# Where the chunk of three row groups stands among a batch's twelve

## The chip, the cores and the metric

The kernel runs on one core of one Trainium2 chip. The metric is the device time of one execution in microseconds (us), lower is better. Each kernel was timed several times beside runs of the kernel before on the same chip. The chip can differ from one set of runs to the next, so each kernel is compared first with the runs beside it.

## The reference

Cross-covariance attention followed by a gated feed-forward layer, cut to what matters:

```python
# q, k, v: (4, 6016, 256); w_gate, w_val: (256, 1536); w_out: (1536, 256)
qn = q / (norm(q, axis=1) + 1e-6);  kn = k / (norm(k, axis=1) + 1e-6)
a  = softmax(kn.transpose(0, 2, 1) @ qn / tau)          # 256 x 256 per batch
x  = (v @ a).reshape(24064, 256)
out = (sigmoid(x @ w_gate) * (x @ w_val)) @ w_out
```

## The kernel before

A batch has 6016 rows, 47 groups of 128. They are worked on in chunks of four groups, so there are twelve chunks and one of them has three groups. The attention matrix of a batch is multiplied into the two weight matrices once (G and H, "gh" in the code), so a chunk needs only v, transposed. A chunk has 12 slots. In each slot TensorE makes a gate and a value block (`glu`), ScalarE takes the sigmoid of the gate, VectorE multiplies. Between these, TensorE does four matmuls of the output projection of the chunk before it, and "side work": the scores of the next batch, with the squares for its norms on VectorE.

```python
groups = [(t, min(TPC, NT - t)) for t in range(0, NT, TPC)]   # TPC = 4, NT = 47
...
def glu(b, ci, f):
    t0, nt = groups[ci]
    n = nt * P
    ...                       # psg and psv have two PSUM banks each
    for ps, w in ((ps_gate, G), (ps_val, H)):
        for ib in range(CB):
            mm(ps[:, :n], w[f // (FG // P)][:, ib, ...], vT[:, ib, :nt, :], ...)
    nc.scalar.activation(out=g_sb[:, :n], in_=ps_gate[:, :n], func=ACT.Sigmoid)
    nc.vector.tensor_tensor(out=hts[b, ci][:, f, :n], in0=ps_val[:, :n], in1=g_sb[:, :n], op=ALU.mult)
...
for b in range(B):
    for ci in range(NCH):
        block = b + 1 < B and ci in (9, 10)
        for f in range(FC):                       # FC = 12 slots
            glu(b, ci, f)
            flush()                               # VectorE copies a finished output row
            if prev is not None and not block:
                out_mms(*prev, f * TPC, (f + 1) * TPC)
            for fn, a in side.get((ci, f), ()):
                fn(*a)
            if (b, ci) == (0, 0) and f < len(gh_order) - 5:
                gh(0, 5 + f, pso, "o")            # 7 of the 12 G/H products of batch 0
        ...                                       # chunks 9 and 10: output matmuls after the slots
        prev = (b, ci)
```

In the first batch nothing hides the loads. The order of the software queue is q and k of the batch, the first v chunk, then the weights.

Of the kernel before, what the change touches and what calls it, by code (L numbers as in the profile page):

```python
# [17 lines left out]
def kernel(  # L18
# [29 lines left out]
    NT = N // P  # L48
# [4 lines left out]
    TPC = 4  # L53
    CH = TPC * P
    NCH = (NT + TPC - 1) // TPC
    groups = [(t, min(TPC, NT - t)) for t in range(0, NT, TPC)]

    head = NT - NT % TPC
    groups0 = groups[: head // TPC] + [(t, n) for t, n in ((head, NT % TPC - 1), (NT - 1, 1)) if n > 0]

    def rows(x, b):
        return x[b].rearrange("(p t) c -> p t c", p=P)
# [24 lines left out]
    def mm(out, lhsT, rhs, start, stop, **kw):  # L87
        nc.tensor.matmul(out, lhsT=lhsT, rhs=rhs, start=start, stop=stop, **kw)  # L88
# [12 lines left out]
    vs = {}  # L101

    def load_v(b, ci):
        t0, nt = groups[ci]
        v_sb = vpool.tile([P, TPC, C], BF16, tag="v", name="v_sb")
        nc.gpsimd.dma_start(out=v_sb[:, :nt, :], in_=rows(v, b)[:, t0 : t0 + nt, :])  # L106
        vs[b, ci] = v_sb


    t0, nt = groups0[0]  # L110
# [20 lines left out]
    for t0, nt in groups0[2:]:  # L131
        load_qk(0, t0, nt)
    load_v(0, 0)

    w_sb = [[consts.tile([P, CB, FG], BF16, name=f"w_{n}{fg}") for fg in range(NFG)] for n in ("gate", "val")]
    w_out_sb = consts.tile([P, FC, C], BF16)
    for fg in range(NFG):
        for w, src in enumerate((moe_w_gate, moe_w_val)):
            nc.gpsimd.dma_start(
                out=w_sb[w][fg],  # L140
                in_=src.rearrange("(t p) f -> p t f", p=P)[:, :, ds(fg * FG, FG)],
            )
    load_v(0, 1)
    nc.gpsimd.dma_start(out=w_out_sb, in_=moe_w_out.rearrange("(t p) c -> p t c", p=P))

# [239 lines left out]

    def transpose_v(b, ci, ps=None, late=None):

        t0, nt = groups[ci]
        v_sb = vs.pop((b, ci))
        vT = vtpool.tile([P, TPC * CB, P], BF16, tag="vT", name="vT")  # L390
        flat = v_sb[:, :nt, :].rearrange("p t c -> p (t c)")
        if ps is None:
            nc.sync.dma_start_transpose(out=vT[:, : nt * CB, :], in_=flat)
        else:
            for n in range(nt * CB):
                nc.tensor.transpose(  # L396
                    out=ps[:, n, :], in_=flat[:, ds(n * P, P)], identity=ident_bf
                )
            half = nt * CB // 2
            (nc.scalar.copy if late is None else late)(vT[:, half : nt * CB, :], ps[:, half : nt * CB, :])  # L400
            nc.vector.tensor_copy(out=vT[:, :half, :], in_=ps[:, :half, :])
        vts[b, ci] = vT.rearrange("p (u cb) n -> p cb u n", cb=CB)
# [1 line left out]
    hts = {}  # L404

    def glu(b, ci, f):
        t0, nt = groups[ci]
        n = nt * P
        G, H = st[b]["gh"]
        vT = vts[b, ci]  # L410
        if f == 0:
            hts[b, ci] = hpool.tile([P, FC, CH], BF16, tag="hT", name="hT")
        ps_gate = psg.tile([P, CH], FP32, tag="g", name="ps_gate")
        ps_val = psv.tile([P, CH], FP32, tag="v", name="ps_val")
        for ps, w in ((ps_gate, G), (ps_val, H)):
            for ib in range(CB):
                mm(
                    ps[:, :n],
                    w[f // (FG // P)][:, ib, ds(f % (FG // P) * P, P)],
                    vT[:, ib, :nt, :],  # L420
                    start=(ib == 0),
                    stop=(ib == CB - 1),
                )
        g_sb = gpool.tile([P, CH], BF16, tag="g", name="g_sb")
        nc.scalar.activation(out=g_sb[:, :n], in_=ps_gate[:, :n], func=ACT.Sigmoid)  # L425
        nc.vector.tensor_tensor(  # L426
            out=hts[b, ci][:, f, :n], in0=ps_val[:, :n], in1=g_sb[:, :n], op=ALU.mult
        )
# [2 lines left out]

    def out_mms(b, ci, n0, n1):

        t0, nt = groups[ci]
        hT = hts[b, ci]
        for n in range(n0, min(n1, nt * FC)):
            s, f = divmod(n, FC)
            if n == 0:
                ffn[b, ci] = opool.tile([P, TPC, C], FP32, tag="osb", name="out_sb")
            if f == 0:  # L440
                ffn["ps"] = pso.tile([P, C], FP32, tag="o", name="ps_o")
            mm(ffn["ps"], hT[:, f, ds(s * P, P)], w_out_sb[:, f, :], f == 0, f == FC - 1)
            if f == FC - 1:
                pending.append((ffn[b, ci], s, ffn["ps"], b, ci))
# [3 lines left out]
    def flush():  # L448
        while pending:
            out_sb, s, ps, b, ci = pending.pop(0)  # L450
            t0, nt = groups[ci]
            nc.vector.tensor_copy(out=out_sb[:, s, :], in_=ps)  # L452
            if s == nt - 1:
                nc.sync.dma_start(out=out_rows[b][:, t0 : t0 + nt, :], in_=out_sb[:, :nt, :])

    def last_rows(b, ci):

        t0, nt = groups[ci]
        s, half = nt - 1, C // 2
        hT = hts[b, ci]  # L460
        nc.sync.dma_start(out=out_rows[b][:, t0 : t0 + s, :], in_=ffn[b, ci][:, :s, :])
        for n, queue in enumerate((nc.sync, nc.scalar)):
            ps = pso.tile([P, half], FP32, tag="o", name="ps_end")
            for f in range(FC):
                mm(ps, hT[:, f, ds(s * P, P)], w_out_sb[:, f, ds(n * half, half)], f == 0, f == FC - 1)
            end = opool.tile([P, half], FP32, tag=f"end{n}", name="end", bufs=1)
            nc.vector.tensor_copy(out=end, in_=ps)  # L467
            queue.dma_start(out=out_rows[b][:, t0 + s, ds(n * half, half)], in_=end)
# [15 lines left out]
    for g, (t0, nt) in enumerate(groups0):  # L484
# [32 lines left out]
    weights(0, 1)  # L517
    late = []
    transpose_v(
        0, 0, psv.tile([P, TPC * CB, P], BF16, tag="v", name="ps_tp"), lambda *a: late.append(a)  # L520
    )
# [12 lines left out]
    def side_work(b):  # L534
# [7 lines left out]
        for ci in range(NCH):  # L542
            nb, nci = (b, ci + 1) if ci + 1 < NCH else (b + 1, 0)
            lb, lci = (b, ci + 2) if ci + 2 < NCH else (b + 1, ci + 2 - NCH)
            if (nb, nci) == (0, 1):
                at(8, lambda: transpose_v(0, 1, psm.tile([P, TPC * CB, P], BF16, tag="m", name="ps_tp")))
            elif nb < B:
                at(ci * FC + 2, transpose_v, nb, nci)
            if lb < B:
                at(ci * FC + 0, load_v, lb, lci)  # L550
# [33 lines left out]
    for b in range(B):  # L584
        side = side_work(b)
        for ci in range(NCH):
            block = b + 1 < B and ci in (9, 10)
            for f in range(FC):
                glu(b, ci, f)
                flush()  # L590
# [5 lines that stand above are left out]
                    gh(0, 5 + f, pso, "o")  # L596
            if prev is not None and block:
                for s in range(TPC):
                    for fn, a in side.get((ci, FC + s), ()):
                        fn(*a)  # L600
                    out_mms(*prev, s * FC, (s + 1) * FC)
                    flush()
            prev = (b, ci)
    for s in range(groups[NCH - 1][1] - 1):
        out_mms(*prev, s * FC, (s + 1) * FC)
        flush()
    last_rows(*prev)


# [33 lines left out]
```

## Time and profile before

| | before |
|---|---|
| time, median of the first 3 runs | 829.4 us |
| span of the profiled run | 827.7 us |
| TensorE busy | 806.9 us, 97% |
| VectorE, ScalarE busy | 71%, 47% |
| first gate matmul of chunk 1, batch 0, from the start of the span | 53.08 us |
| from there to the end | 774.6 us |

With TensorE busy for 97%, shares tell nothing of a change that moves work about. What can be read is the start of each matmul in the timeline. The next start less the time that the columns between take (0.423 ns a column in this kernel) is a gap. After the first 40 us this kernel has four gaps of 0.04 us or more (0.25, 0.30, 0.30 and 0.07). Where a group in the listing has an odd count, a record is missing, and the apparent gap of one matmul (0.22 us) there is not a real one.

### The profile page before, as it was taken

How to read it: one execution, taken by the hardware profiler on the slowest of the kernel's cores; microseconds unless marked ns; L12 is line 12 of the kernel's file. 1: busy time of each engine (PE TensorE's matmuls, PEld its weight loads, DVE VectorE, ACT ScalarE, POOL GpSimd, SP SyncE). 2: the span in 40 equal slices, each digit the busy share in tenths (PEclk: the TensorE clock that was granted, in tenths of full speed). 3: DMA queues.
4: the chain of work that ended last, by engine and by line, in shares of the span. 5: the costliest groups of instructions: out<-in, count | busy, mean ns of one | idle time of the engine just before them, and what ended most of it. 6: DMA issues, size and time to landing. Idle time of an engine off the chain costs nothing.

```text
span 827.7 us, 13626 instructions
## 1 busy us (share of the span) xinstructions
PE 806.9 (97%) x5122; PEld 498.5 (60%) x5134; DVE 591.5 (71%) x1027; ACT 390.8 (47%) x642; POOL 83.1 (10%) x159
## 2 busy tenths in 40 slices
PE   4799999999999999999999999999999999999998
PEld 2456666665665666665575666666566566666666
DVE  6777877787667777778767777777766666666665
ACT  4554444446644444445654444444655444444442
POOL 5532100002210100000311010000000000000000
PEclk9899999999999999999999999999999999999999
DMA  9999623226746443223876452223322323322211
GB/s 210 206 201 216 110 52 90 60 53 136 158 88 119 96 89 61 54 52 85 158 138 124 80 107 60 51 63 75 64 61 63 73 52 85 60 58 69 47 36 71
DMA packets 79026, 77.17 MB, mean 93 GB/s; under 512 B 50800, under 2 KB 55920, under 8 KB 78960
## 3 DMA queue, kind: packets, MB, share of 16 engines
q0 software_dynamic: 23920, 38.81, 28.1%
q1 hardware_dynamic: 54752, 36.91, 17.4%
q8 instruction: 40, 0.66, 0.3%
q10 hardware_dynamic: 288, 0.59, 0.2%
q14 instruction: 26, 0.21, 0.1%
HBM read 78.64 MB, written 24.64 MB: 125 GB/s over the span
## 4 chain that ended last, share of the span: by engine, by line
PE 94%; DMA 4%; DVE 1%; issue 0%; ACT 0%; POOL 0%; POOLq 0%
PE ps_o L88 30%; PE ps_gate L88 29%; PE ps_val L88 29%; PE ps_s L88 4%; DMA k_sb<-in_k_dram 3%; PE ps_gh L88 2%; DMA w_gate<-in_moe_w_gate_dram 1%; DVE hT L426 0%; ACT g_sb L425 0%; PE ps_end L88 0%; DVE sq L176 0%; PE ps_n L88 0%; POOL q_sb L97 0%; PE ps_tp L396 0%; DVE end L467 0%
## 5 line engine op out<-in xcount | busy, mean ns | idle before, releaser
L426 DVE TENSOR_TENSOR hT<-ps_val,g_sb 128x512 bf16<-128x512 f32 (+1 forms) x576 | 390.8, 679 | 205.6 <-ACT g_sb L425 201.0
L425 ACT ACTIVATE g_sb<-ps_gate 128x512 bf16<-128x512 f32 (+1 forms) x576 | 338.2, 588 | 386.2 <-PE ps_gate L88 380.2
L88 PE MATMUL ps_val<-vT,gh_H 128*128 128x512 bf16 (+1 forms) x1152 | 337.6, 375 | 0.3
L88 PE MATMUL ps_gate<-vT,gh_G 128*128 128x512 bf16 (+1 forms) x1152 | 337.5, 375 | 0.2
L88 PE MATMUL ps_o<-w_out_sb,hT 128*128 128x256 bf16 x2244 | 324.9, 273 | 0.0
L88 PEld LDWEIGHTS <-hT 128*128 128x128 bf16 x2268 | 221.0, 98 | 124.6
L88 PEld LDWEIGHTS <-gh_H 128*128 128x128 bf16 x1152 | 112.7, 98 | 132.1 <-issue 1.4
L88 PEld LDWEIGHTS <-gh_G 128*128 128x128 bf16 x1152 | 112.4, 98 | 37.6 <-ACT gh_G L379 0.2
L106 POOL DMA_DIRECT2D v_sb<-in_v_dram x48 | 25.5, 531 | 620.2 <-DMA vT<-v_sb 480.4
L452 DVE COPY out_sb<-ps_o 128x256 f32<-128x256 f32 x187 | 77.2, 413 | 12.6 <-PE ps_o L88 12.6
L88 PE MATMUL ps_s<-k_sb,q_sb 128*128 128x256 bf16 x376 | 70.5, 289 | 15.8 <-DMA k_sb<-in_k_dram 8.8
L88 PEld LDWEIGHTS <-q_sb 128*128 128x128 bf16 x376 | 38.6, 103 | 24.6 <-issue 9.6
L215 DVE TENSOR_TENSOR acc<-acc,sq 128x1024 bf16<-128x1024 bf16 (+1 forms) x66 | 44.1, 669 | 0.0
L176 DVE TENSOR_TENSOR sq<-q_sb 128x1024 bf16<-128x1024 bf16 (+2 forms) x44 | 29.3, 667 | 0.0
L97 POOL DMA_DIRECT2D q_sb<-in_q_dram x48 | 26.5, 552 | 15.2 <-DMA q_sb<-in_q_dram 7.3
L97 POOL DMA_DIRECT2D k_sb<-in_k_dram x48 | 26.2, 545 | 16.1 <-DMA k_sb<-in_k_dram 6.6
L176 DVE TENSOR_TENSOR sq<-k_sb 128x1024 bf16<-128x1024 bf16 (+2 forms) x34 | 22.4, 658 | 0.2 <-DMA k_sb<-in_k_dram 0.2
L174 ACT ACTIVATE sq<-k_sb 128x1024 bf16<-128x1024 bf16 (+1 forms) x11 | 11.2, 1019 | 13.6 <-DMA k_sb<-in_k_dram 13.6
L88 PE MATMUL ps_gh<-w_val,e_sb 128*128 128x512 bf16 x45 | 13.5, 379 | 0.2
L88 PEld LDWEIGHTS <-e_sb 128*128 128x128 bf16 x112 | 10.2, 98 | 5.3 <-DMA w_gate<-in_moe_w_gate_dram 0.6
L88 PE MATMUL ps_gh<-w_gate,e_sb 128*128 128x512 bf16 x41 | 12.7, 379 | 0.7 <-DMA w_gate<-in_moe_w_gate_dram 0.5
L425 ACT ACT_TABLE_LOAD x6 | 7.7, 1283 | 9.0 <-PE ps_gate L88 9.0
(69 smaller groups left out, 121.1 us busy)
## 6 DMA issues: line engine op xcount, KB each, us to landing
out_dram<-out_sb SPq DMA_DIRECT2D x44, 512.0 KB, 2.9
v_sb<-in_v_dram POOLq DMA_DIRECT2D x44, 256.0 KB, 3.8
q_sb<-in_q_dram POOLq DMA_DIRECT2D x43, 256.0 KB, 7.4
k_sb<-in_k_dram POOLq DMA_DIRECT2D x43, 256.0 KB, 8.1
out_dram<-out_sb SPq DMA_DIRECT2D x3, 384.0 KB, 3.1
w_gate<-in_moe_w_gate_dram POOLq DMA_DIRECT2D x3, 256.0 KB, 8.0
w_val<-in_moe_w_val_dram POOLq DMA_DIRECT2D x3, 256.0 KB, 8.1
w_out_sb<-in_moe_w_out_dram POOLq DMA_DIRECT2D x1, 768.0 KB, 13.3
```

What stands on the lines that cost most here:

```text
L88: nc.tensor.matmul(out, lhsT=lhsT, rhs=rhs, start=start, stop=stop, **kw)
L97: nc.gpsimd.dma_start(out=tl[:, :nt, :], in_=rows(src, b)[:, t0 : t0 + nt, :])
L106: nc.gpsimd.dma_start(out=v_sb[:, :nt, :], in_=rows(v, b)[:, t0 : t0 + nt, :])
L174: nc.scalar.activation(out=sq[:, :nt, :], in_=src[:, :nt, :], func=ACT.Square)
L176: engine.tensor_tensor(out=sq[:, :nt, :], in0=src[:, :nt, :], in1=src[:, :nt, :], op=ALU.mult)
L215: nc.vector.tensor_tensor(out=acc[:, :nt, :], in0=acc[:, :nt, :], in1=st[b]["sq", w][:, :nt, :], op=ALU.add)
L425: nc.scalar.activation(out=g_sb[:, :n], in_=ps_gate[:, :n], func=ACT.Sigmoid)
L426: nc.vector.tensor_tensor(out=hts[b, ci][:, f, :n], in0=ps_val[:, :n], in1=g_sb[:, :n], op=ALU.mult)
L452: nc.vector.tensor_copy(out=out_sb[:, s, :], in_=ps)
```

## The change

The intent is that the partial chunk comes first and the last chunk of each batch is a full one. Loads of q and k keep their groups.

```diff
+    short = NT - (NCH - 1) * TPC
+    chunks = [(0, short)] + [(short + t * TPC, TPC) for t in range(NCH - 1)]
...
     def load_v(b, ci):
-        t0, nt = groups[ci]
+        t0, nt = chunks[ci]
...   (the same line in transpose_v, glu, out_mms, flush and last_rows)
-    for s in range(groups[NCH - 1][1] - 1):
+    for s in range(chunks[NCH - 1][1] - 1):
```

More of the change, by code (lines that the diff above doesn't have):

```diff
@@ L386, in transpose_v @@
     def transpose_v(b, ci, ps=None, late=None):
-        t0, nt = groups[ci]
+        t0, nt = chunks[ci]
         v_sb = vs.pop((b, ci))
@@ L406, in glu @@
     def glu(b, ci, f):
-        t0, nt = groups[ci]
+        t0, nt = chunks[ci]
         n = nt * P
@@ L432, in out_mms @@
     def out_mms(b, ci, n0, n1):
-        t0, nt = groups[ci]
+        t0, nt = chunks[ci]
         hT = hts[b, ci]
@@ L450, in flush @@
             out_sb, s, ps, b, ci = pending.pop(0)
-            t0, nt = groups[ci]
+            t0, nt = chunks[ci]
             nc.vector.tensor_copy(out=out_sb[:, s, :], in_=ps)
@@ L456, in last_rows @@
     def last_rows(b, ci):
-        t0, nt = groups[ci]
+        t0, nt = chunks[ci]
         s, half = nt - 1, C // 2
```

## The prediction

> **What bounds the kernel now.** I read the page's busy times first, then the chain of waits, then the groups with shapes kept apart, and last the timeline at the head, at a batch's edge and at the tail. The first part of the page, and the sums by engine of its chain:
>
> ```profile
> PE 806.9 (97%) x5122; PEld 498.5 (60%) x5134; DVE 591.5 (71%) x1027; ACT 390.8 (47%) x642; POOL 83.1 (10%) x159
> ...
> PE 94%; DMA 4%; DVE 1%; issue 0%; ACT 0%; POOL 0%; POOLq 0%
> ```
>
> TensorE is busy for 97% and carries 94% of the chain; the 4% of DMA is the head, where q and k of the first batch arrive. So the question is not how busy anything is, but where TensorE stands still. Walking the TensorE timeline start by start (the next start minus the columns streamed), I find 19.4 us of gaps. About 16.2 us lie before 38.9 us, nearly all waits for q, k and the first weight. After that the real gaps are 0.25 us at 42.0, 0.30 at 254.0 and 0.30 at 453.5, some of 0.03 to 0.07, and about 2 us that are only missing records (0.21 us, each beside a group with an odd count). The groups by form:
>
> ```profile
> L426 DVE TENSOR_TENSOR hT<-ps_val,g_sb 128x512 bf16<-128x512 f32 x528 | 364.1, 690 | 181.5 <-ACT g_sb L425 179.5 <-PE ps_gate L88 0.4
> L425 ACT ACTIVATE g_sb<-ps_gate 128x512 bf16<-128x512 f32 x528 | 315.1, 597 | 368.4 <-PE ps_gate L88 368.4
> L426 DVE TENSOR_TENSOR hT<-ps_val,g_sb 128x384 bf16<-128x384 f32 x48 | 26.7, 555 | 24.0 <-ACT g_sb L425 21.4 <-PE ps_gh L88 2.2
> L425 ACT ACTIVATE g_sb<-ps_gate 128x384 bf16<-128x384 f32 x48 | 23.1, 487 | 17.8 <-PE ps_gate L88 11.8 <-DVE hT L426 6.0
> ```
>
> The x48 forms are the short chunks, 12 slots in each of 4 batches. ScalarE and VectorE wait for TensorE in both sizes.
>
> **Cost of TensorE work, from starts.** In the steady part pairs of 512-column matmuls start 0.433 us apart, pairs of 384 columns 0.325 and groups of four of 256 columns 0.433. All are 0.423 ns per column, with nothing to see per instruction. A full slot of gate and value is 4 x 0.2165 = 0.866 us, a short one 4 x 0.1625 = 0.650 us, four output matmuls 0.433 us.
>
> **What the Trainium skill says.** "TensorE: Matmul & The Clock Gate", section "Back-to-back issue gap", gives N / 2.4 + 2.5 ns when warm: 215.8, 162.5 and 109.2 ns for 512, 384 and 256 columns. The trace has 216.5, 162.5 and 108.3, so it agrees; the 131 ns that the same section has for a sustained stream at 512 is not met here. "VectorE: DVE Perf Modes", section "The TRN2 errata — SBUF-src ops pay a fixed extra latency per instruction", gives (120 + columns) / 0.96 ns for a PSUM source: 658 and 525 ns; the trace has 690 and 555 for the product, 30 more, but the slope agrees, so a short slot does not take three quarters of a full one's VectorE time. "ScalarE: Activation LUTs", section "What ACT_TABLE_LOAD costs", gives 1283 ns for the load and 1380 for a drain; the trace shows 1283 and the next activation 0.01 us later, so I use 1.28 us. "DMA: Bandwidth & Descriptors", section "Queues, rings and completion order", says that an SDMA engine takes the descriptors of a ring in ring order. The head agrees: k tiles of the same queue land 2.48 us apart (waits ending at 28.31 and 30.79), so a tile issued earlier and made smaller moves up all behind it.
>
> **The change, part by part.** The rows per batch are the same 47. Each batch's chunk 0 loses 12 slots x 4 matmuls x 128 columns x 0.423 ns = 2.60 us of gate and value work and its last chunk gains as much. The output work moves too, and sums to the same. Number and shapes of instructions are unchanged, only their order. For a kernel with TensorE full that is zero, so what is left is four edges.
>
> (1) *Head, the load.* The first v tile is queued before the first weight tile, and that weight is what starts the G/H matmuls:
>
> ```profile
> 28.51 8.00 DMA w_gate<-in_moe_w_gate_dram
> 36.55 0.60 PE ps_gh L88 x2
> ...
> 40.89 0.60 ACT g_sb L425
> 41.51 0.70 DVE hT L426
> 42.26 0.59 PE ps_val L88 x2
> ```
>
> A tile of four rows costs 2.48 / 2 = 1.24 us of the queue, so a row less lands the weight 0.31 us earlier. The first G/H matmul would start at 36.24; its operand e, ready at 35.85, allows it. Six transposes in place of eight save nothing: TensorE waits for e after them.
>
> (2) *Head, the first chunk.* There are no output matmuls yet. After the weight the chain goes through ScalarE: two copies of G and H, the table load 39.59 to 40.87, the sigmoid, the product, and only then the value matmul of slot 2. With all 0.31 earlier and the short forms: sigmoid 40.57 to 41.06, product 41.09 to 41.65, value of slot 2 at 41.71, against 42.26. That is 0.55 us earlier. But TensorE does 5 short pairs (2 slots and a gate) x 0.108 = 0.54 us less before it, so there is no gain: the wait there grows from 0.25 to some 0.4 (and 0.1 at the gate before it). Then the G/H slots: TensorE 0.650 + 0.433 = 1.083 us; VectorE 0.555 + 0.743 / 2 = 0.93 us, ScalarE 0.487 + 0.687 / 2 = 0.83. TensorE bounds them, but the product of slot 1 is behind a G/H scaling, and I allow 0.1 us. The five slots without G/H take 0.650 us. There the loop gate (0.49 from start to end), sigmoid (0.04 + 0.487), product (0.03 + 0.555) and release (0.05) is 1.65 us, while the value matmul two slots on wants its bank 2 x 0.650 + 0.325 = 1.625 us after the gate's start; with full slots it was 2.06. So no slack is left, and the copies of the second chunk's transposes, 0.58 us on ScalarE and 0.42 on VectorE in slot 8, fall into this. I work it out to 0.22 us of wait in slot 11. Sum of (1) and (2): -0.01 + 0.1 + 0.22, about **+0.35 us**.
>
> (3) *Batch edges.* Output matmuls are handed out four a slot, so a predecessor of three rows leaves slots 9 to 11 without any. Today these are in chunk 0:
>
> ```profile
> 252.64 0.41 DVE L452 COPY out_sb<-ps_o 128x256 f32<-128x256 f32 x1
> 252.97 0.68 DVE L176 TENSOR_TENSOR sq<-q_sb 128x1024 bf16<-128x1024 bf16 x1
> 253.57 1.28 DVE L426 TENSOR_TENSOR hT<-ps_val,g_sb 128x512 bf16<-128x512 f32 x2
> ...
> 254.31 0.59 PE L88 MATMUL ps_val<-vT,gh_H 128*128 128x512 bf16 x2
> ```
>
> The last output copy and a square stand ahead of the product of slot 10, whose value bank the next chunk's first slot needs. The gate matmuls before it started at 253.58 and take 0.43, so TensorE loses 0.30 us. This occurs after chunk 0 of batches 1 and 2, and not in batch 3, whose VectorE has no next batch to prepare. After the change the three slots are in chunk 1, with scores and squares in the same slots, and batch 0 has them too. So three losses in place of two: **+0.30 us**. The short chunk 0 of later batches has its 48 output matmuls: TensorE 0.650 + 0.433 + 0.108 (scores) = 1.19 us a slot, VectorE 0.555 + 0.14 (output) + 0.34 (squares) = 1.03, no wait. The last chunk, now full, has the G/H matmuls as well and only gains slack.
>
> (4) *Tail.* The end is the same two half rows, their copies and transfers. One more row of output matmuls stands before them, which the sum counts. The transfer just ahead carries three rows, not two. The page has 2.0 us to landing for 256 KB and 2.9 for 512 KB, so 0.45 us more; it is issued 1.2 us before the last, and some of it may hold that up: **+0.1 us**.
>
> Sum: 0.35 + 0.30 + 0.1 = 0.75 us; 829.4 + 0.7 = **830.1 us**.
>
> **The rivals.** *The head pays.* If the weight 0.31 us earlier, and less work before the wait in slot 2, came out whole, and the short slots ran without the wait that I give them, the time would be about 829. Against it: work taken from chunk 0 comes back in chunk 11, while waits that hang on ScalarE's table load do not shrink with it. *The two-bank loop binds the whole short chunk.* If each of the 12 slots of the first chunk lost 0.1 to 0.15 us, this would make 831 to 831.5. For it is the slack of none in the last five slots; against it that the G/H slots have 0.15 us over VectorE's time. *The edge stalls vanish* rather than move, because chunk 1 meets other neighbours: 0.9 us less than my sum, 829.2; the unchanged slot parity of squares and scores speaks against it. *A late load.* The first DMA transpose takes 16.0 us to land, from 48.84; its chunk starts about 2.3 us earlier than today's 71.5, which leaves some 4 us. Were it late, all of that would be lost; I give it 3%.
>
> **Range and chances.** Each of the four terms can be off by its own size, and runs of the kernel before differ by 0.4 us. 829.1 to 831.2 holds these. A change of 2% is 16.6 us, more than the whole of the idle time after the head, and the head's loads are not shortened by more than 0.31. Faster 0.5%, within 98.5%, slower 1%.
>
> **What would show it.** In the changed profile: first G/H matmul near 36.24; chunk 1's first gate near 50.8 (53.08 today, less 2.60 by work alone would be 50.48); a gap of 0.3 us at the end of chunk 1 in batches 0, 1 and 2 and none at the end of chunk 0; TensorE busy time within 1 us; the same half-row tail. It is wrong if gaps appear inside the later short chunks, or if a transfer ends TensorE's wait after 55 us.

## The result

The changed kernel took 830.40 us (median of 6 runs, 830.02 to 830.76), the kernel before 829.54 (6 runs, 829.36 to 829.76). The ratio is 1.001, 95% interval 0.9997 to 1.0023. A ratio is the mean time of one kernel's runs over that of the other's in the same rounds, so it is not quite the ratio of the medians quoted. No run of either kernel falls in the range of the other.

Busy times and the chain's shares by engine, after:

```profile
PE 807.5 (97%) x5120; PEld 498.5 (60%) x5132; DVE 591.3 (71%) x1027; ACT 390.7 (47%) x642; POOL 83.2 (10%) x159
...
PE 93%; DMA 4%; DVE 1%; ACT 1%; issue 1%; POOL 0%; ACTq 0%; POOLq 0%
```

Nothing to see, as one would expect: the same work. (The two matmuls fewer are missing records.) ScalarE has entered the chain with 1%. The groups by form, after; the columns are busy us and mean ns of one, then idle time ahead and what ended it:

```profile
L429 DVE TENSOR_TENSOR hT<-ps_val,g_sb 128x512 bf16<-128x512 f32 x528 | 364.1, 690 | 190.3 <-ACT g_sb L428 188.6
L428 ACT ACTIVATE g_sb<-ps_gate 128x512 bf16<-128x512 f32 x528 | 314.8, 597 | 361.1 <-PE ps_gate L91 361.0
L429 DVE TENSOR_TENSOR hT<-ps_val,g_sb 128x384 bf16<-128x384 f32 x48 | 26.5, 556 | 16.0 <-ACT g_sb L428 15.7
L428 ACT ACTIVATE g_sb<-ps_gate 128x384 bf16<-128x384 f32 x48 | 23.4, 490 | 24.1 <-DVE hT L429 12.5 <-PE ps_gate L91 11.4
```

Counts and durations are those of before, to 3 ns, so no instruction became dearer. The difference is in waits. The chain through the head, after (start, duration, what; L533 is the sigmoid's table load):

```profile
28.64 7.88 DMA w_gate<-in_moe_w_gate_dram
36.51 0.05 issue
36.56 0.61 PE ps_gh L91 x2
...
38.31 0.69 ACT gh_G L382
39.00 0.58 ACT gh_H L382
39.58 0.02 issue
39.59 1.28 ACT L533
40.88 0.01 issue
40.89 0.50 ACT g_sb L428
41.39 0.02 issue
41.41 0.57 DVE hT L429
41.98 0.04 issue
42.02 0.48 PE ps_val L91 x2
```

Behind the first G/H matmuls and a row sum, up to the value matmul of slot 2, the chain no longer runs over TensorE. It runs over a copy of G and the inverse of that row sum on VectorE (left out above), the two copies on ScalarE, the table load, the sigmoid and the product. It ends 0.24 us earlier than before (42.26), while TensorE has 0.54 us less to do. The batch's edge, after, in the timeline of chunk 1 of batch 0:

```profile
66.06 0.41 DVE L455 COPY out_sb<-ps_o 128x256 f32<-128x256 f32 x1
...
66.39 0.68 DVE L179 TENSOR_TENSOR sq<-q_sb 128x1024 bf16<-128x1024 bf16 x1
...
66.99 1.28 DVE L429 TENSOR_TENSOR hT<-ps_val,g_sb 128x512 bf16<-128x512 f32 x2
67.00 0.59 PE L91 MATMUL ps_gate<-vT,gh_G 128*128 128x512 bf16 x2
...
67.73 0.59 PE L91 MATMUL ps_val<-vT,gh_H 128*128 128x512 bf16 x2
```

This is the pattern of before, copy and square ahead of the product that frees a value bank: 67.00 + 0.43 = 67.43, the value matmul starts at 67.73, 0.30 us are lost. It recurs at 267.8 and 467.3, so three times in place of two.

The account of the two profiled runs, from starts in the timelines:

| stretch | before | after | difference | less the work moved |
|---|---|---|---|---|
| start to the spreading of the k norms (`ps_rk`, a matmul) | 34.16 | 34.33 | +0.17 | (head of the run, untouched) |
| from there to the first G/H matmul | 2.39 | 2.23 | -0.16 | -0.16 |
| from there to chunk 1's first gate | 16.53 | 14.84 | -1.69 | -1.69 + 2.60 = +0.91 |
| from there to the end | 774.62 | 777.40 | +2.78 | +2.78 - 2.60 = +0.18 |

The last +0.18 is the third edge gap of 0.30 less one small gap of 0.07 us (at 606.98 before) that this run has not; the remaining 0.05 is no more than the rounding of the spans to 0.1 us. The sum is 827.7 to 828.8 us of span. The profiled run of the changed kernel is the slowest of its six.

### The profile page after: what moved, and what is told of

Same layout as the page of the kernel before. It is cut to its first block, busy times and chain, and to the rows that moved or that the text cites. A ratio compares the mean times of both kernels' runs of the same rounds, so it can differ in the third digit from the quotient of the medians.

```text
span 828.8 us, 13622 instructions
## 1 busy us (share of the span) xinstructions
PE 807.5 (97%) x5120; PEld 498.5 (60%) x5132; DVE 591.3 (71%) x1027; ACT 390.7 (47%) x642; POOL 83.2 (10%) x159
## 4 chain that ended last, share of the span: by engine, by line
PE 93%; DMA 4%; DVE 1%; ACT 1%; issue 1%; POOL 0%; ACTq 0%; POOLq 0%
PE ps_o L91 30%; PE ps_val L91 29%; PE ps_gate L91 29%; PE ps_s L91 4%; DMA k_sb<-in_k_dram 3%; PE ps_gh L91 2%; DMA w_gate<-in_moe_w_gate_dram 1%; DVE hT L429 1%; ACT g_sb L428 0%; DVE sq L179 0%; PE ps_end L91 0%; ACT L533 0%; PE ps_n L91 0%; DVE gh_G L384 0%; ACT gh_G L382 0%
## 5 line engine op out<-in xcount | busy, mean ns | idle before, releaser
L177 ACT ACTIVATE sq<-k_sb 128x1024 bf16<-128x1024 bf16 (+1 forms) x11 | 11.2, 1018 | 13.6 <-DMA k_sb<-in_k_dram 13.6
```

What stands on the lines that cost most here:

```text
L177: nc.scalar.activation(out=sq[:, :nt, :], in_=src[:, :nt, :], func=ACT.Square)
```

## The experiments

Theory A is the account above: the short first chunk of batch 0 loses 0.91 us in waits and gains a little from an earlier weight; each stretch of slots without output matmuls that also carries squares costs 0.30 us; the rest is neutral. The rivals put the loss in the short chunks of the later batches (B), deny that the gaps cost anything in the end (C), hold slots without output matmuls to be dear by themselves (D), or hold the short chunk to be bound as a whole by its loop of gate, sigmoid, product and freed bank, so that a cured wait comes back elsewhere (E). The differences are below 0.2% for every kernel here. What decides between the theories is therefore where the gaps stand in the one profile of each kernel; the times only have to agree.

**Batch 0 alone has the short chunk first.**

```diff
-    chunks = [(0, short)] + [(short + t * TPC, TPC) for t in range(NCH - 1)]
+    at_front = [(0, short)] + [(short + t * TPC, TPC) for t in range(NCH - 1)]
+    chunks_of = [at_front] + [groups] * (B - 1)        # read as chunks_of[b][ci]
```

> Batch 0 has its short chunk first as in the changed kernel, batches 1 to 3 have it last as before. Theory A (the loss is made of a head term of about 0.75 us in the first chunk and 0.30 us for each stretch of three slots without output matmuls that carries next-batch squares): chunk 1 of batch 0 starts near 51.4 us as in the changed kernel; a 0.30 us gap at the end of chunk 1 of batch 0 and at the end of chunk 0 of batch 2, none in batch 1; two gaps, so about 0.3 us less than the changed kernel and 0.7 more than before, 830.2. Rival B (the loss is spread over the short first chunks of batches 1 to 3, none of it in the head): about 829.6. Rival C (gaps at the edges cost nothing in the end because later slack takes them up): as long as the changed kernel, 830.4.

Measured: 830.15 us median (mean of 5 runs 830.17) beside 829.65 (mean of 9 runs 829.67). The gaps are where A has them: 0.30 us after the group that starts at 66.72, none in batch 1, 0.30 at 453.7. From the first G/H matmul to chunk 1 it is 14.84 us, as in the changed kernel. So the head's loss is in batch 0 and nothing is lost in the later short chunks; B falls. Its median is 0.25 us below the changed kernel's 830.40, where A expects 0.3, but the spreads of the two overlap and they were not run side by side.

**Three output matmuls per slot after a chunk of three.** The same edit in the changed kernel and in the kernel before (there with `groups`):

```diff
-                    out_mms(*prev, f * TPC, (f + 1) * TPC)
+                    rows_prev = chunks[prev[1]][1]
+                    out_mms(*prev, f * rows_prev, (f + 1) * rows_prev)
```

> The changed kernel, with a three-row predecessor's 36 output matmuls handed out three per slot over twelve slots in place of four per slot over nine. Theory A: the three 0.30 us gaps at the end of chunk 1 of batches 0, 1 and 2 are gone and nothing comes in their place, so 0.9 us less than the changed kernel, near 829.5, level with before; chunk 1 still starts near 51.4. Rival C (the gaps cost nothing, or come back as smaller waits in the nine slots that now have one matmul less): no gain, 830.4.

> The kernel before with the same three per slot after a three-row chunk. Theory A: its two 0.30 us gaps (254.0 and 453.5) are gone, 0.6 us less than before, near 828.9. Rival C: no gain, 829.5.

Measured: 829.44 us (829.28 to 829.72) for the changed kernel so edited, 829.05 (828.71 to 829.17) for the kernel before so edited, beside the same 829.65. The 0.30 us gaps are gone in both timelines and none has come in their place. From chunk 1 to the end it is 776.50 us in place of 777.40, and 773.96 in place of 774.62. These are 0.90 and 0.66 us, of which the gaps are 0.90 and 0.60. So the gaps cost their full length, and C falls.

**The short chunk as the eighth of twelve.**

```diff
+    at_7 = [(t * TPC, TPC) for t in range(7)] + [(7 * TPC, short)] + [(7 * TPC + short + t * TPC, TPC) for t in range(NCH - 8)]
+    chunks_of = [at_7] * B
```

> The chunk of three row groups is the eighth of the twelve in each batch, so the slots without output matmuls fall into the last three of the ninth, where VectorE has no next-batch work, and both the head and the tail have full chunks. Theory A (it takes squares in these slots to make the 0.30 us gap): no gap at the batch edges and none in the ninth chunk, head as before (chunk 1 near 53.1), 0.6 us less than before, near 828.9. Rival D (slots without output matmuls lose time by themselves): four gaps of about 0.3 us at the end of the ninth chunks, 830.0 or more.

Measured: 829.09 us (828.77 to 829.16), beside 829.65. The last three slots of the ninth chunk, in batch 0 around 183 to 185 us, have no output matmuls and no squares, and no gap:

```profile
183.50 0.42 DVE L457 COPY out_sb<-ps_o 128x256 f32<-128x256 f32 x1
...
183.83 1.48 DVE L431 TENSOR_TENSOR hT<-ps_val,g_sb 128x512 bf16<-128x512 f32 x2
...
184.22 0.59 PE L93 MATMUL ps_gate<-vT,gh_G 128*128 128x512 bf16 x2
...
184.65 0.60 PE L93 MATMUL ps_val<-vT,gh_H 128*128 128x512 bf16 x2
```

The value matmul follows its gate after 0.43 us, as it should. The output copy is there and does no harm alone. So D falls. That it takes the square as well is read from VectorE's order at the gaps; these slots also lack the next batch's scores, and no run has one without the other. Head and remainder are as A has them: 16.52 us from the first G/H matmul to chunk 1, and 773.97 to the end. This kernel and the kernel before with three per slot have lower medians than both kernels of this study. All their runs lie below all runs of the kernel before, but at 0.07% the intervals (0.998 to 1.0005, and 0.9979 to 1.0004) don't exclude 1.

**The largest new wait of the first chunk.** Within the 0.91 us, the wait that the prediction did not have is in slot 8, after:

```profile
47.36 0.56 DVE L429 TENSOR_TENSOR hT<-ps_val,g_sb 128x384 bf16<-128x384 f32 x1 [0.48 <-ACT g_sb L428]
...
47.84 0.74 DVE L384 TENSOR_SCALAR gh_H<-ps_gh,rrow 128x512 bf16<-128x512 f32 x1
48.12 0.33 PE L91 MATMUL ps_val<-vT,gh_H 128*128 128x384 bf16 x1
...
48.63 0.34 PE L91 MATMUL ps_val<-vT,gh_H 128*128 128x384 bf16 x1 [0.19 <-DVE gh_H L384]
```

Slot 8 is the first to use the last third of H, whose second half is the twelfth G/H product, made in slot 6. Its scaling stands in VectorE's order behind the product of slot 6 and ends at 48.58. The second value matmul could have started 0.16 us after the first, at 48.28, and starts at 48.63: 0.35 us. The experiment makes that product in slot 5, in a free PSUM bank:

```diff
-                if (b, ci) == (0, 0) and f < len(gh_order) - 5:
+                if (b, ci) == (0, 0) and f < len(gh_order) - 6:
                     gh(0, 5 + f, pso, "o")
+                    if f == len(gh_order) - 7:
+                        gh(0, 6 + f, pss, "s")
```

It ran beside the changed kernel itself, which was run once more:

> The changed kernel once more, as the measure for the three beside it on the same chip: 830.4 us, 14.85 us from the first G/H matmul to the first gate matmul of chunk 1.

> The changed kernel with the last of the twelve G/H products made one slot of the first chunk earlier, in a PSUM bank of its own, so that its VectorE copy is done before the value matmul of slot 8 wants it. Theory A (0.33 us of the 0.91 that the short first chunk loses is the wait for that copy): the wait in slot 8 goes, 14.5 us from the first G/H matmul to chunk 1, 0.35 us less than the changed kernel, 830.05. Rival E (TensorE is held by the loop through ScalarE and VectorE as a whole, and the wait in slot 8 is only where it shows): the loss turns up in slots 9 to 11, no gain.

Measured: 830.53 us (mean 830.52) for the changed kernel, 830.20 (mean 830.16) for the edit, beside 829.68 for the kernel before. From the first G/H matmul to chunk 1 it is 14.51 us in place of 14.84. The wait in slot 8 is gone, and slot 11 waits 0.20 us as before. So the 0.33 us were a wait of their own, and E fails for it. The medians differ by the same 0.33 us, with overlapping spreads.

**The size of the first v load.**

```diff
+        ld = TPC if (b, ci) == (0, 0) else nt
-        nc.gpsimd.dma_start(out=v_sb[:, :nt, :], in_=rows(v, b)[:, t0 : t0 + nt, :])
+        nc.gpsimd.dma_start(out=v_sb[:, :ld, :], in_=rows(v, b)[:, t0 : t0 + ld, :])
```

> The changed kernel, but the first v load brings four row groups as before, of which three are used. If the smaller load is worth 0.31 us, as the prediction had it, the first G/H matmul comes 0.31 us later counted from the spreading of the k norms than in the changed kernel run beside it, and the time is 0.3 us more; from the traces so far (2.25 to 2.39 us with four rows, 1.76 to 2.30 with three) some 0.2 us, and the time the same within what five rounds can tell.

Measured: 830.89 us (mean 830.78) beside 830.53 (mean 830.52) of the changed kernel, with overlapping spreads. From the spreading of the k norms to the first G/H matmul it took 2.29 us here and 1.77 in the changed kernel beside it. Over all the profiles, four rows gave 2.39, 2.25, 2.29 and 2.29 us, three rows 2.23, 2.30, 1.76, 2.37, 1.77 and 1.77. The means are 2.31 and 2.03, a difference of 0.27 us, but it comes as half a microsecond or nothing. The landings in the traces say more. Counted from the spreading of the k norms, the v tile lands at -0.19 to -0.21 us with four rows and at -0.45 to -0.53 with three: some 0.29 earlier, close to the 0.31 predicted. The weight behind it does not follow: it lands at 2.20 to 2.35 with four rows, at 2.18 to 2.33 in three of the profiles with three rows, and at 0.80 to 0.83 in the other three. The same transfer with three rows, in the changed kernel's first profile (issued at 28.64) and its second (28.53):

```profile
w_gate<-in_moe_w_gate_dram POOLq DMA_DIRECT2D x1, 256.0 KB, 7.9
w_gate<-in_moe_w_gate_dram POOLq DMA_DIRECT2D x1, 256.0 KB, 6.4
```

So the weight is 1.4 us earlier or not at all, and of the 1.4 only half a microsecond is used, because the first matmul on the operand e does not start before 1.70 in any profile. What decides which was not found. Nor is it shown that the row less has a part in it: three in six against none in four is what chance alone gives one time in six (an estimate, 20 of the 120 ways to place three).

**All cures in one.** Three per slot, the twelfth product in slot 5, and the transposes for chunk 1 moved from slot 8 to the slot that it left:

```diff
-                at(8, lambda: transpose_v(0, 1, psm.tile(...)))
+                at(6, lambda: transpose_v(0, 1, psm.tile(...)))
```

> The changed kernel with three cures together: output matmuls of a three-row predecessor three per slot, the last G/H product one slot earlier, and the transposes for chunk 1 in slot 6 in place of slot 8. Theory A: 0.90 + 0.33 + 0.21 us of gaps go, 829.0, so that the short chunk first is no longer dearer than last; 14.3 us from the first G/H matmul to chunk 1. Rival E: only the 0.90 goes, 829.5.

Measured: 829.43 us (mean 829.50), beside 829.68 for the kernel before and 830.53 for the changed one. This is a miss by 0.4 us, and E's number. The trace tells two reasons. The transposes cost slot 9 the same 0.20 us that they had cost slot 11 (14.47 us from the first G/H matmul to chunk 1, not 14.3), so for this wait E was right. And there is a new wait at the first gate of chunk 3, for a DMA that landed late. The timeline of this kernel, and the DMA view's issue-to-landing time (last column) of the transpose issued at 68.91:

```profile
68.91 1.75 SPq L396 DMA_TRANSPOSE vT<-v_sb  x1
...
83.52 0.11 PEld L91 LDWEIGHTS <-gh_G 128*128 128x128 bf16 x2 [0.41 <-DMA vT<-v_sb]
```

```profile
vT<-v_sb SPq DMA_TRANSPOSE x1, 14.6
```

68.91 + 14.6 = 83.5 us. In the kernel before the same transpose is issued at 72.77 and takes 10.8, landing at 83.6; in the changed kernel it is 66.98 + 16.5 = 83.5; with the changed kernel's three per slot 69.30 + 13.6 = 82.9. It lands at nearly one time, whenever it is issued (82.9 to 84.0 in all ten profiles), while the DMA engines are full with the next batch's q and k (their share is 1.0 to 1.1 in this stretch in both kernels). Before, chunk 3 starts at about 87.1, 3.5 us later. In the changed kernel it starts at about 84.4, less than 1 us later, and in the kernel with the twelfth product in slot 5 only 0.3 us later. In this one it would have started at 83.23, and loses 0.30.

## Why the prediction was right

It was right: 830.4 us against 830.1, inside the range. The edges came out as reasoned, and so did the head's waits as far as it saw them. That the sum is so close has luck in it: a wait of 0.35 us that it did not see is as large as its whole term for the head, and was in part made up by a tail term that came to nothing and a small gap that went.

- **The work is conserved.** Shown: durations and counts are unchanged, and every difference found is a wait. TensorE's busy time is within the 1 us given (806.9 and 807.5).
- **(1) The weight comes 0.31 us earlier.** Right for the v tile (some 0.29), not shown for the weight. The first G/H matmul was 0.16 earlier in the profiled run and 0.27 on the average of ten profiles, but each profile shows one of two places and not a shift by 0.31: it was at 36.56 in the profiled run and at 35.95 in the repeated one, on either side of the 36.24 expected. So the step from "in ring order" to "moves up all behind it" failed: the section that the prediction cites for the order also says that a later transfer can finish its write before an earlier one, and here the place in the queue did not fix the time of landing.
- **(2) The first chunk.** The waits came to 0.91 us from the first G/H matmul on; the prediction's figures amount to some 0.62. (Its sum -0.01 + 0.1 + 0.22 is 0.31, which it rounded up to 0.35.) Up to slot 2 it has 0.30 (0.54 of work less, 0.24 of time, from 0.55 less the load's 0.31), and 0.29 was measured. The 0.1 it allowed for the G/H slots was 0.04. The 0.22 of slot 11 was 0.20. What it lacked is the 0.35 us of slot 8. It checked G/H slots for throughput, VectorE's 0.93 us against TensorE's 1.083, and not for the deadline of the last product, which short slots bring closer. So the term of +0.35 us measured 0.91 less what the load gave: 0.75 in the profiled runs, and 0.91 - 0.27 = 0.64 with the average of the profiles. Two slips change nothing in the sum: the lines that it shows have VectorE wait for ScalarE's sigmoid (179.5 of 181.5 us), not for TensorE directly, and with full slots the bank is wanted 2 x 0.866 + 0.433 = 2.165 us after the gate's start, not 2.06.
- **(3) Batch edges, +0.30.** Right to the hundredth, with places and batches. That the stalls move rather than vanish was shown, no gap came inside the later short chunks, and the spreading and the eighth-chunk kernels bear out the cause.
- **(4) Tail, +0.1.** Wrong: nothing. From the issue of the last transfer to the end of the span it is 827.7 - 824.83 = 2.87 us before and 828.8 - 825.94 = 2.86 after. The larger transfer ahead did not hold up the last one.
- **Sum.** 0.64 + 0.30 + 0, and -0.12 for the rest of the last stretch, is 0.82 us; the medians differ by 0.86, and by 0.85 when the changed kernel was run again.
- **The rivals.** *The head pays* and *the edge stalls vanish* did not happen. *The two-bank loop binds the whole short chunk* has a grain of truth: slots 9 to 11 have no slack, and a wait cured there comes back. *A late load* was nearer than the 3% given it suggests: the transpose to watch was the second, not the first, with less than 1 us to spare. The prediction's 4 us for the first is a misreading: its chunk, chunk 2, starts at 69.99 before, not at 71.5, and at 67.00 after. It comes 3.0 us earlier, not 2.3, because a chunk of three rows also leaves its successor 12 x 0.108 = 1.3 us less of output work. The transpose landed at 64.74, so 2.3 us were left. No transfer ended a wait of TensorE after 55 us in the changed kernel.

## What to carry to other kernels

Where one engine is full and the work is only reordered, add up the waits at the few edges where its neighbours have no slack: shrinking work there gains less than its size (1.69 of 2.60 us here), and the same work comes back in full elsewhere. In this kernel the partial chunk did best where the slots that it leaves without filler carry no other engine's extra work, or with its filler spread evenly over the slots; each took some 0.6 us off the median. When slots shrink, check deadlines as well as throughput: operands made a fixed number of slots ahead, and transfers that land at one time however early they are issued.

## What the Trainium skill lacked or had wrong

- "TensorE: Matmul & The Clock Gate", section "Back-to-back issue gap": the 131 ns per matmul of 512 columns in a sustained stream is not met; 216.5 ns in all of this kernel, with weight loads between, which is the page's figure for a single gap.
- "ScalarE: Activation LUTs", section "What ACT_TABLE_LOAD costs": no drain of 1380 ns shows. The load takes 1.28 us from 39.59 and the sigmoid starts at 40.88 in the kernel before and 40.89 in the changed one.
- "VectorE: DVE Perf Modes", section "The TRN2 errata — SBUF-src ops pay a fixed extra latency per instruction": the table's 120 cycles are too few for a product from PSUM; 690 ns at 512 columns and 555 at 384 give 150 (690 x 0.96 - 512; 555 x 0.96 - 384 is 149). The same section has a figure that fits below the table, (N + 151) / 0.96 for an fp32 `tensor_tensor` add, which gives 691 and 557; the prediction's "30 more" is the difference of the two.
- "DMA: Bandwidth & Descriptors": no section has the time of a DMA transpose beside a full software queue. It took 10.8 to 16.5 us here and landed at 82.9 to 83.6 us in four kernels, though issued up to 5.8 us apart; the median over a run was 3.7.
- On no page: why the first weight lands in one of two places, 1.4 us apart, in runs of one kernel (0.8 or 2.2 to 2.4 us after the norms are spread; first G/H matmul at 1.77 or 2.2 to 2.4).
